# One block of 512 columns for batch 0's two halves in the up layer's last chunk, and new ranks in the planner

## The chip, the cores and the metric

The kernel runs on one core of a Trainium2 chip. A core has a matrix engine (TensorE, PE in the rows; its weight loads are PEld), VectorE (DVE), ScalarE (ACT), GpSimd (POOL) and SyncE (SP), which issues most DMAs. Each engine takes its own queue of instructions in order and waits on semaphores for the others. The metric is the device time of one execution in microseconds (us), the median of several runs. One execution is profiled, and its rows are what the argument rests on.

## What is computed

The reference is attention with a decay, followed by two feed-forward layers, all in float32:

```python
scores = q @ k^T / sqrt(64) + cum[i] - cum[j]      # cum: running sum of log f; causal
attn = softmax(scores); x = attn @ v               # 4 batches, 8 heads, 576 positions, 64 wide
x = x.transpose(0, 2, 1, 3).reshape(2304, 512)
x = (x @ w_a * (x @ w_b)) @ w_out                  # 512 -> 1536 -> 512: the up and down layers
h = x @ w_in                                       # 512 -> 1024
solu = h * softmax(h); ln = (solu - mean) / sqrt(var + 1e-6) * g_ln
out = ln @ w_out2                                  # 1024 -> 512
```

The kernel reaches float32 accuracy by parts: most operands are split into a high and a low part, and three products (high with high, low with high, high with low) are added in PSUM.

## The kernel before

**Stages.** The heads of batch 0 are worked in two passes, rows 0 to 255 of all 8 heads (kind `K0`) and then rows 256 to 575 (kind `K1`), so that the up layer can start on the first half early. The other 24 heads are whole (`KE` for the first two of batch 1, `KF` for the rest). Each head has: transposes of q and k (line 982), splits into high and low (lines 1003 to 1026), scores for the row maximum (line 1054) with a maximum on VectorE (line 1081 or 1084), the maximum turned into a row (lines 1099 and 1108), the scores with everything in them (line 1130), the exponential (ACT, lines 1192 and 1254) with the causal mask on GpSimd (line 1263), its split (lines 1272 and 1278), the product with v (lines 1215 and 1313) and the division by the sum (lines 1343 to 1378).

**The causal mask of the maximum.** For a head whose number is below `Y["PM"]` (and for all of `K0` and `K1`) TensorE adds the mask by a small bf16 matmul on each diagonal block (`ident` by `cmask`, line 1054), and VectorE takes a plain maximum (line 1081). For the others VectorE adds the mask and takes the maximum in one custom instruction and a read of its accumulator (line 1084).

**The up layer.** `STR` lists blocks of tokens: 0 and 1 are the two halves of batch 0 with 256 tokens each, 2 and 3 are 512 tokens of batches 1 and 2. For every block `i` and every chunk `c` of 128 of the 1536 features there is a unit (`up_unit`): 12 matmuls for `w_a` and 12 for `w_b`, on 256 or 512 columns, into two PSUM banks (line 1441); ACT copies the first out (line 1464), VectorE multiplies it with the second (line 1466), and SP stores the product to a DRAM tile `gs`. Units have a low rank, `key + Y["UK"]`: TensorE takes them where no attention work is ready. The 12 weight chunks are loaded, repaired (lines 699 to 715) and split (lines 737 and 742) before that. Batch 3, with the last 64 rows of every batch, goes through Strassen products instead ("group", line 1803, with prepared sums of weights, lines 1725 and 1732). Then come the down layer (`down`, line 2008), which loads `gs` again, and per pair of token blocks the last layers (lines 2096, 2162 to 2231 and 2241).

**The planner.** The order of all queues is not written out. Every operation is recorded with a rank (`key`) and the engines that may do it, and `Sched.run` plays a list schedule with rough costs: on each engine the ready operation of the lowest rank goes next, and where two or three engines may do it, the one that would end first, with a lean of so many us (`BIAS`, `BL`, `BS` ...). The ranks come from the table `Y`: shifts by head (`ZD`), by stage of a head (`KP`, `KN`), by weight (`WK`), and so on. `PN` is the first of the later layers' 28 weight blocks that is converted early and parked in DRAM.

**Fillers.** Where the planner's own schedule leaves TensorE a gap of more than `Y["FG"]` us, before `F1` = 640 us, a run of bf16 matmuls on constants is put into its queue (line 2321). Their number is the gap times `Y["FF"]` over the cost of one:

```python
if gap > Y["FG"] and place(at):
    todo.append((at, fill(gap * Y["FF"], *place(at), ...)))
```

Of the kernel before, what the change touches and what calls it, by code (L numbers as in the profile page):

```python
# [8 lines left out]
F32 = mybir.dt.float32  # L9
# [66 lines left out]
class Sched:  # L76
# [227 lines left out]
    "PN": 25,  # L304
    "KK": 265.3196,
    "KD": 15.1517,
    "TLD": 14.6185,
    "XP": -30.9366,
    "TO": 44.2857,
    "PA": 2.1045,  # L310
    "PS": 5.9662,
    "TK": 127.6384,
    "TD": 31.9136,
    "BT": -0.044,
    "UP": 434.967,
    "PG": 4.0796,
    "BP": -0.2335,
    "QK": 2,
    "TWK": 9.8272,
    "TWQ": 11.1039,  # L320
    "BK": -0.37,
    "BM": 0.9846,
    "Z0": 9.8683,
    "T0": 6.3669,
    "T1": 6.2527,
    "TA": 11.7627,
    "TF": 20.0998,
    "U0": 1.5861,
    "U1": 2.8457,
    "UF": 2.2924,  # L330
    "UL": 0.128,
    "LEAD": (1.2596, 5.9871),
    "SHRINK": 1.7818,
    "W0": 51.1769,
    "WD0": 5.2376,
    "WN": 3,
    "WD1": 0.0,
    "WD2": 15.5982,
    "EZ": 7.505,
    "EO": 20.0045,  # L340
    "TE": 28.4496,
    "DL": 0,
    "BIAS": 0.9425,
    "UO": (8.3054, 8.9928, 13.3396),
    "UD": 95.319,
    "UK": 380.0568,
    "L3": 18,
    "TL": (0.0, 0.0),
    "F1": 640.0,
    "FG": 0.3661,  # L350
    "FF": 0.7794,
# [3 lines left out]
    "YC": 17.6302,  # L355
    "T2": 11.7517,
    "TB": 1,
    "HB": 0,
    "F2": 181.8536,
    "LATE": 0.1776,  # L360
# [26 lines left out]
    "WIN": 0.0013,  # L387
# [4 lines left out]
def kernel(  # L392
# [48 lines left out]
          for i, (_, q0, q1) in enumerate(STR)]  # L441
    gsp = [dram.tile([P, 2 * TN], F32, name=f"gsp_{c}") for c in range(NF)]
# [986 lines left out]
    def up_unit(i, c, key, last):  # L1429
        b, q0, q1 = STR[i]  # L1430
        n_ = q1 - q0
# [3 lines left out]
        u[0].lo = 3 if i >= Y["L3"] else 2  # L1435
        uo = (0, n_) if len(u) == 1 else (0, 0)
# [14 lines left out]
        for j, (m, ks) in enumerate(parts):  # L1451
            rx = [(xsb[i][p], (s, p)) for p in ks for s in "hl"]
# [5 lines left out]
        aw = 2 * P if i < 2 else XT  # L1458
# [124 lines left out]
    def unit_plan(i, z0, dz):  # L1583
        for c in range(NF):
# [8 lines left out]
    unit_plan(0, xz[0] + 3.0, Y["U0"])  # L1593
# [776 lines left out]
```

## Time and profile before

| | us |
|---|---|
| median of 3 runs | 889.82 (889.47 to 891.45) |
| profiled execution, its own time | 887.92 |
| its span from the first to the last instruction | 886.04 |
| TensorE busy in it | 869.9 |
| fillers in that | 21.1 |

Rows name a line, an engine, an operation, what it writes and reads (tile names), its shape and its count. "[0.50 <-ACT xrw L1343]" says that the engine stood idle for 0.50 us before, and that ACT's instruction of line 1343 ended this. Matmuls overlap, so the distance of their starts is what one costs, and the time in a row is longer by the last one's own length.

### The profile page before, as it was taken

How to read it: one execution, taken by the hardware profiler on the slowest of the kernel's cores; microseconds unless marked ns; L12 is line 12 of the kernel's file. 1: busy time of each engine (PE TensorE's matmuls, PEld its weight loads, DVE VectorE, ACT ScalarE, POOL GpSimd, SP SyncE). 2: the span in 40 equal slices, each digit the busy share in tenths (PEclk: the TensorE clock that was granted, in tenths of full speed). 3: DMA queues.
4: the chain of work that ended last, by engine and by line, in shares of the span. 5: the costliest groups of instructions: out<-in, count | busy, mean ns of one | idle time of the engine just before them, and what ended most of it. 6: DMA issues, size and time to landing. Idle time of an engine off the chain costs nothing.

```text
span 886.0 us, 14300 instructions
## 1 busy us (share of the span) xinstructions
PE 869.9 (98%) x4899; PEld 755.7 (85%) x4899; DVE 676.4 (76%) x1305; ACT 444.9 (50%) x856; POOL 295.4 (33%) x440
## 2 busy tenths in 40 slices
PE   7999999999999999999999999999999999999997
PEld 5788989998888888888899987888888888888886
DVE  7988778789878867764788899887785666668774
ACT  3798755655654545444445556643532443344243
POOL 5666757656534533122234341112110010003001
PEclk9999999999999999999999999999999999999999
DMA  4476844445454453121276656421111212111001
GB/s 104 125 207 191 225 123 129 126 122 133 118 152 122 133 155 92 55 71 49 93 247 224 217 176 228 150 68 55 53 48 48 73 36 71 37 38 52 20 25 36
DMA packets 113356, 98.02 MB, mean 111 GB/s; under 512 B 69730, under 2 KB 92900, under 8 KB 113284
## 3 DMA queue, kind: packets, MB, share of 16 engines
q1 hardware_dynamic: 111396, 96.37, 36.9%
q10 hardware_dynamic: 1888, 0.75, 0.4%
q8 instruction: 38, 0.62, 0.3%
q14 instruction: 34, 0.28, 0.1%
HBM read 64.33 MB, written 26.49 MB: 103 GB/s over the span
## 4 chain that ended last, share of the span: by engine, by line
PE 87%; DVE 7%; ACT 2%; issue 2%; DMA 1%; POOL 0%; SPq 0%; DVEq 0%; ACTq 0%
PE ps L1441 20%; PE ps L2008 17%; PE ps L2241 10%; PE ps L2096 9%; PE ps L1803 9%; PE ps L1313 6%; PE ps L1130 5%; PE ps L1054 3%; PE ps L1215 3%; PE ps L2225 2%; PE ps L982 2%; DVE sets L1026 1%; DVE mts L1081 1%; PE ps L2321 1%; DMA sets<-sets 1%
## 5 line engine op out<-in xcount | busy, mean ns | idle before, releaser
L1441 PE MATMUL ps<-xs,wt 128*128 128x256 f32 (+1 forms) x1152 | 221.8, 341 | 0.5 <-POOL wt L742 0.5
L1441 PEld LDWEIGHTS ps<-xs,wt 128*128 128x128 f32 x1152 | 177.9, 189 | 21.8 <-POOL wt L742 0.8
L2008 PE MATMUL ps<-xs,wt 128*128 128x512 f32 (+1 forms) x360 | 81.2, 372 | 0.6 <-DVE fw L1853 0.5
L2008 PE MATMUL ps<-VS,wt 128*128 128x512 f32 (+1 forms) x360 | 79.5, 370 | 0.0
L2241 PE MATMUL ps<-sets,pexp 128*128 128x512 f32 x238 | 73.5, 390 | 0.0
L2008 PEld LDWEIGHTS ps<-xs,wt 128*128 128x128 f32 x360 | 62.5, 188 | 12.6 <-DVE fw L1853 1.6
L2008 PEld LDWEIGHTS ps<-VS,wt 128*128 128x128 f32 x360 | 62.9, 188 | 11.3
L1130 PE MATMUL ps<-sets 128*128 128x288 f32 (+16 forms) x400 | 68.8, 309 | 1.5 <-DVE mts L1084 0.5
L1313 PE MATMUL ps<-pexp,VS 128*128 128x448 f32 (+4 forms) x396 | 64.3, 311 | 0.0
L1130 PEld LDWEIGHTS ps<-sets 128*128 128x128 f32 (+2 forms) x400 | 58.3, 191 | 5.8 <-DMA sets<-sets 1.1
L1084 DVE CUSTOM_DVE_ANT_0 ps<-ps,cmask 128x512 f32<-128x512 f32 (+4 forms) x110 | 59.0, 553 | 5.3 <-PE ps L1054 2.3
L1263 POOL TENSOR_SCALAR_AFFINE_SELECT fw<-fw 128x128 f32<-128x128 f32 (+1 forms) x120 | 35.1, 322 | 80.5 <-ACT fw L1254 80.3
L1313 PEld LDWEIGHTS ps<-pexp,VS 128*128 128x128 f32 x396 | 58.7, 190 | 3.1 <-DVE pexp L1278 0.2
L1254 ACT ACTIVATE fw<-ps 128x768 f32<-128x768 f32 (+1 forms) x48 | 40.0, 838 | 26.1 <-PE ps L1130 24.9
L2241 PEld LDWEIGHTS ps<-sets,pexp 128*128 128x128 f32 x238 | 44.3, 188 | 9.0
L2241 PE MATMUL ps<-sets,xs 128*128 128x512 f32 x119 | 46.3, 389 | 0.0
L1054 PE MATMUL ps<-sets 66*128 66x512 f32 (+4 forms) x192 | 42.9, 323 | 3.3 <-DMA sets<-xs 1.7
L1272 ACT CAST pexp<-fw 128x768 fp32r<-128x768 f32 (+1 forms) x44 | 37.5, 859 | 14.4 <-POOL fw L1263 11.5
L2096 PE MATMUL ps<-wt,VS 128*128 128x512 f32 x162 | 44.3, 391 | 0.0
L1278 DVE TENSOR_TENSOR pexp<-fw,pexp 128x768 fp32r<-128x768 f32 (+1 forms) x35 | 36.2, 1043 | 9.1 <-ACT pexp L1272 8.8
L2109 DVE TENSOR_TENSOR xrw<-ps,xrw 128x512 f32<-128x512 f32 x34 | 23.5, 690 | 24.0 <-PE ps L2096 24.0
L1464 ACT COPY fw<-ps 128x256 f32<-128x256 f32 (+1 forms) x48 | 23.0, 479 | 37.3 <-PE ps L1441 31.4
(278 smaller groups left out, 1870.8 us busy)
## 6 DMA issues: line engine op xcount, KB each, us to landing
fw<-in_moe_w_out_dram SPq DMA_DIRECT2D x16, 512.0 KB
tdr<-fw SPq DMA_DIRECT2D x12, 512.0 KB
gs<-fw SPq DMA_DIRECT2D x24, 256.0 KB
sets<-sets SPq DMA_DIRECT2D x42, 144.0 KB
xrw<-tdr SPq DMA_DIRECT2D x11, 512.0 KB
fw<-in_moe_w_a_dram SPq DMA_DIRECT2D x10, 512.0 KB
fw<-in_moe_w_b_dram SPq DMA_DIRECT2D x10, 512.0 KB
nat<-in_k_dram SPq DMA_DIRECT2D x35, 128.0 KB
```

The source lines that it names most:

```text
L1054: nc.tensor.matmul(bank(ms[part], o, w), lhsT=a, rhs=b, start=o // 512 not in opened, stop=stop, skip_group_check=True)
L1084: nc.vector.tensor_tensor_reduce(out=x, in0=x, in1=cmask[:n, off:off + w], scale=1.0, scalar=-3.0e38, op0=ALU.add, op1=ALU.max, accum_out= ...
L1130: nc.tensor.matmul(bank(ss[i], o, w), lhsT=a, rhs=b, start=o // 512 not in opened, stop=stop, skip_group_check=True)
L1254: op(("ACT", t_act(n, True)), key + K.rk[4] + 5.5 + 0.9 * i, lambda i=i, n=n, pf=pf: nc.scalar.activation(out=pf(), in_=bank(ss[i], K.base ...
L1272: op(("ACT", t_act(n)), key + K.rk[5] + 6.8 + 0.9 * i, lambda bh=bh, n=n, pf=pf: nc.scalar.copy(out=pexp[:, 64 * bh.slot:64 * bh.slot + n] ...
L1278: o.fn = lambda o=o, bh=bh, bl=bl, n=n, pf=pf: ENG[o.eng].tensor_tensor(out=pexp[:, 64 * bl.slot:64 * bl.slot + n], in0=pf(), in1=pexp[:, ...
L1313: nc.tensor.matmul(bank(u, K.uo + q0, q1 - q0), lhsT=V[:, vp], rhs=src[:, o:o + q1 - q0], start=(k_ in K.first and ip == 0), stop=(k_ in K ...
L1441: nc.tensor.matmul(bank(u[m % len(u)], uo[m], n_), lhsT=wv(m, wp, c)[:, kk], rhs=xsv(i, xx, kk), start=(kk == 0 and n == 0), stop=(kk == K ...
L1803: nc.tensor.matmul(bank(bk, 0, TN), lhsT=operand(w, wp, kk), rhs=xb(x, xp)[:, kk], start=(first and kk == 0 and n == 0), stop=(kk == 1 and ...
L2008: nc.tensor.matmul(bank(py[d], 0, n), lhsT=WO[c][0][:, wp * DM:(wp + 1) * DM][:, ds_], rhs=ghv(gb, gp)[:, :n], start=(c == 0 and i == 0), ...
L2096: nc.tensor.matmul(bank(bk, 0, 512), lhsT=yc(yx, yp)[:, kk], rhs=wi(wx, wp, kk), start=(n == 0), stop=(n == 5))
L2241: nc.tensor.matmul(bank(po, 0, DM), lhsT=(zhv, zhv, zlv)[i][:, c], rhs=w2(c, (0, 1, 0)[i]), start=(c == 0 and i == 0), stop=(c == NF2 - 1 ...
```

## The change

**The wide block.** With `CM` = 11, the units of blocks 0 and 1 are made for chunks 0 to 10 alone. Chunk 11 of both is one unit with `i` = -1 and 512 columns: its moving operand `xsm` takes both halves of the split x in one access, its product goes to a new DRAM tile `gsm`, and the down layer's chunk 11 of batch 0 reads this by one DMA in place of two. It is planned behind the last weighing of the `KE` heads, since its 512-column buffers lie where these keep their data.

**The table.** Nearly all ranks and leans are new. Four entries do more than shift: `PM` 10 to 11 (head 10 gets its mask on TensorE), `PN` 25 to 26 (one weight block fewer is converted early), and `FG` 0.3661 to 0 with `FF` 0.7794 to 0.8938 (every gap gets fillers, and a larger share of it). `L3` and `HB` change too, but no operation reads them differently.

```diff
 Y = {
+    "CM": 11,
-    "PN": 25,
+    "PN": 26,
...
-    "UK": 380.0568,
+    "UK": 405.8544,
...
-    "FG": 0.3661,
-    "FF": 0.7794,
+    "FG": 0.0,
+    "FF": 0.8938,
...
-    "PM": 10,
+    "PM": 11,
...
+    gsm = [dram.tile([P, XT], F32, name=f"gsm_{c}") for c in range(NF)]
...
+    def xsm(part, p):
+
+        o = 2 * 2 * P * p + part * 2 * P
+        return xs[:, :2 * XH].rearrange("p (a x) -> p a x", a=2)[:, :, o:o + 2 * P]
...
     def up_unit(i, c, key, last):
-        b, q0, q1 = STR[i]
-        n_ = q1 - q0
+        both = i < 0
+        n_ = XT if both else STR[i][2] - STR[i][1]
...
-                        bank(u[m % len(u)], uo[m], n_), lhsT=wv(m, wp, c)[:, kk], rhs=xsv(i, xx, kk),
+                        bank(u[m % len(u)], uo[m], n_), lhsT=wv(m, wp, c)[:, kk],
+                        rhs=xsm(xx, kk) if both else xsv(i, xx, kk),
...
-        af = K1W + KEW + UPS if i == 2 else ()
+        af = K1W + KEW + UPS if both or i == 2 else ()
+        to = gsm[c] if both else gs[i][c]
...
-    unit_plan(0, xz[0] + 3.0, Y["U0"])
-    unit_plan(1, max(xz[1] + 3.0, xz[0] + 3.0 + 12 * Y["U0"]), Y["U1"])
+    CM = int(Y["CM"])
+    unit_plan(0, xz[0] + 3.0, Y["U0"], range(CM))
+    zm = max(xz[1] + 3.0, xz[0] + 3.0 + 12 * Y["U0"])
+    unit_plan(1, zm, Y["U1"], range(CM))
+    NKE = sum(1 for _, K in JOBS if K is KE) * len(KE.wei)
+    zk = max([Z[j] + Y["UO"][2] for j, x in enumerate(JOBS) if x[1] is KE] + [zm])
+    unit_plan(-1, zk + 0.02, Y["U1"], range(CM, NF))
...
+    merged = [(lambda c: gsm[c], XT, (-1,))]
...
-            for pi, (src, w, parts) in enumerate(blocks[j]):
+            bl = merged if j == 0 and c >= CM else blocks[j]
+            for pi, (src, w, parts) in enumerate(bl):
```

What it does to the queues is seen at three places. The lines after the change lie 7 to 17 higher for the same code (1441 is now 1449, 1054 is 1061, 2321 is 2338).

**TensorE, where the up layer goes from 256 to 512 columns** (some 205 us into the span). `xs` is the split x, `wt` the weights, `sets` the split q and k, `pexp` and `VS` the weights and v of a head. Before:

```order
L1441 MATMUL ps<-xs,wt 128x256 x6
L1313 MATMUL ps<-pexp,VS 128x128 x3
L1313 MATMUL ps<-pexp,VS 128x448 x3
L1313 MATMUL ps<-pexp,VS 128x192 x3
L1441 MATMUL ps<-xs,wt 128x256 x6
L1441 MATMUL ps<-xs,wt 128x512 x6
L1108 MATMUL ps<-ident,mts 7x128
L1054 MATMUL ps<-sets 128x512
L1054 MATMUL ps<-sets 128x384
L1054 MATMUL ps<-sets 128x128
```

and now:

```order
L1061 MATMUL ps<-sets 128x512
L1449 MATMUL ps<-xs,wt 128x512 x6
L1061 MATMUL ps<-sets 128x256 x2
L1061 MATMUL ps<-sets 128x320
L1061 MATMUL ps<-sets 128x384
L1061 MATMUL ps<-sets 128x128
L1449 MATMUL ps<-xs,wt 128x512 x12
L1320 MATMUL ps<-pexp,VS 128x128 x3
L1320 MATMUL ps<-pexp,VS 128x448 x3
L1320 MATMUL ps<-pexp,VS 128x192 x3
L1115 MATMUL ps<-ident,mts 7x128
L1449 MATMUL ps<-xs,wt 128x512 x6
```

Before, the last narrow matmuls are followed by the first of batch 1; now the narrow ones end earlier, and the 24 wide ones of chunk 11 (6, 12 and 6) stand between the scores and the products of heads, ahead of batch 1's.

**ACT, around 35 us**, in the pass from the first half's heads to the second's: line 1355 copies a head's result out of PSUM, line 1020 makes the high part of the next head's q. Before:

```order
L1003 CAST sets<-ps 64x576
L1363 ACTIVATE xrw<-xrw 128x256
L1366 ACTIVATE xrw<-xrw 128x256
L1355 COPY xrw<-ps 64x256
L1020 ACTIVATE sets<-ps 64x320
L699 ACTIVATE fw<-fw 128x512
```

and now (line 1027 is 1020, line 1362 is 1355):

```order
L1010 CAST sets<-ps 64x576
L1370 ACTIVATE xrw<-xrw 128x256
L1373 ACTIVATE xrw<-xrw 128x256
L1027 ACTIVATE sets<-ps 64x320
L1362 COPY xrw<-ps 64x256
L706 ACTIVATE fw<-fw 128x512
```

The high part of q stands ahead of the copy.

**TensorE, the scores for the maximum of head 10** (`cmask`, `ident`: the mask as a matmul). Before:

```order
L1054 MATMUL ps<-sets 128x512
L1054 MATMUL ps<-sets 128x384
L1054 MATMUL ps<-sets 128x128
L1054 MATMUL ps<-sets 128x256 x2
L1054 MATMUL ps<-sets 128x320
L1130 MATMUL ps<-sets 128x448 x2
L1130 MATMUL ps<-sets 128x64 x2
```

and now, from the second of its score matmuls on:

```order
L1061 MATMUL ps<-sets 128x384
L1061 MATMUL ps<-sets 128x128
L1061 LDWEIGHTS ident
L1061 MATMUL ps<-cmask,ident 128x128
L1061 LDWEIGHTS ident
L1061 MATMUL ps<-cmask,ident 128x128
L1061 MATMUL ps<-sets 128x256 x2
L1061 MATMUL ps<-sets 128x320
L1061 LDWEIGHTS ident
L1061 MATMUL ps<-cmask,ident 128x128
L1061 LDWEIGHTS ident
L1061 MATMUL ps<-cmask,ident 128x64
```

Five mask matmuls, one on each diagonal block (four are in these rows), with their loads of `ident`, stand between the scores.

Fillers are 107 matmuls before and 136 now. In the part of the queue that took the first 45 us before there are 67 of them before (8 of 512 columns, 48 of 352, 11 of 256) and 86 now (9, 61 and 16); behind it 40 before and 50 now, all of 352 columns. The first 330 rows of TensorE's queue, fillers aside, are the same but for two swaps.

## Rows read from the trace of the kernel before

**Rows 1.** The page's part 1: busy us, share, instructions by engine.
```profile
PE 869.9 (98%) x4899; PEld 755.7 (85%) x4899; DVE 676.4 (76%) x1305; ACT 444.9 (50%) x856; POOL 295.4 (33%) x440
```

**Rows 2.** Stages: length, busy us (instructions) by engine, granted clock, DMA share, GB/s.
```profile
0.00:45.00 45.00, 38.88 (x266) 28.94 (x267) 37.70 (x90) 25.33 (x58) 27.00 (x68) 1.00 0.47 118
45.00:110.00 65.00, 64.90 (x480) 58.29 (x480) 53.15 (x84) 54.69 (x107) 46.15 (x53) 1.00 0.75 207
110.00:440.00 330.00, 326.91 (x1973) 290.85 (x1972) 247.39 (x495) 174.91 (x288) 148.32 (x228) 1.00 0.39 110
440.00:560.00 120.00, 118.00 (x634) 109.00 (x633) 104.68 (x180) 62.91 (x129) 40.55 (x52) 1.00 0.66 218
560.00:866.00 306.00, 306.00 (x1483) 256.78 (x1482) 224.93 (x445) 120.06 (x262) 30.45 (x30) 1.00 0.17 53
866.00:886.00 20.00, 15.17 (x73) 11.85 (x72) 8.57 (x16) 7.00 (x14) 2.88 (x10) 1.00 0.15 39
```

**Rows 3.** The same stages, instructions of line 2321 alone: the fillers; their sum.
```profile
0.00:45.00 45.00, 13.77 (x67) 6.63 (x67) 1.00 0.47 118
...
sum 886.00, PE 21.11 PEld 10.07; mean PE 3.52 PEld 1.68
```

**Rows 4.** TensorE's waits from 45 us on: us in total, times, longest.
```profile
PE ps L1803 <- ACT fw L1818: 0.8, 2, 0.6
PE ps L1803 <- ACT nat L1818: 0.6, 1, 0.6
PE ps L1108 <- DVE mts L1084: 0.5, 1, 0.5
```

**Rows 5.** The chain that ended last: start us, us, what.
```profile
100.46 2.88 PE ps L1441 x24
...
418.22 19.06 PE ps L1441 x84
```

**Rows 6.** Timeline of TensorE (start us, us, instruction, count), 24 and 36 us.
```profile
24.13 0.29 PE L1054 MATMUL ps<-cmask,ident 128*128 128x128 bf16 x2
24.25 0.61 PE L2321 MATMUL ps<-cmask,ident 128*128 128x352 bf16 x3
24.60 0.74 PE L1130 MATMUL ps<-sets 128*128 128x256 f32 x2
...
36.22 0.47 PE L1054 MATMUL ps<-sets 66*128 66x512 f32 x1 [0.32 <-ACT sets L1020]
...
37.30 0.68 PE L1130 MATMUL ps<-sets 128*128 128x256 f32 x4
```

**Rows 7.** Timeline of TensorE at fillers and at what waits behind them.
```profile
1.58 3.59 PE L2321 MATMUL ps<-fw 128*128 128x512 bf16 x8 [1.58 <-DVE fw L600]
...
11.70 0.41 PE L1054 MATMUL ps<-sets 66*128 66x256 f32 x2 [1.22 <-DMA sets<-xs]
...
27.68 0.48 PE L1215 MATMUL ps<-xrw,fw 128*128 128x256 f32 x1 [0.50 <-ACT xrw L1343]
...
214.42 1.80 PE L2321 MATMUL ps<-cmask,ident 128*128 128x352 bf16 x11
216.77 0.28 PE L1108 MATMUL ps<-ident,mts 128*7 128x128 f32 x1 [0.54 <-DVE mts L1084]
```

**Rows 8.** Timeline of ACT, then of VectorE, around 36 us.
```profile
35.23 0.35 ACT L1355 COPY xrw<-ps 64x256 f32<-64x256 f32 x1
35.60 0.43 ACT L1020 ACTIVATE sets<-ps 64x320 fp32r<-64x320 f32 x1
...
37.27 2.21 DVE L1081 TENSOR_REDUCE mts<-ps 128x1 f32<-128x512 f32 x4
```

**Rows 9.** Line 1278, the weights' low part: ns min/median/max by engine; who waited.
```profile
L1278 DVE TENSOR_TENSOR pexp<-fw,pexp x35: 937/960/2110, 194.7 to 412.4; 128x768 fp32r<-128x768 f32 x18, 128x832 fp32r<-128x832 f32 x17
L1278 POOL TENSOR_TENSOR pexp<-fw,pexp x9: 1840/1976/2430, 141.0 to 263.2; 128x832 fp32r<-128x832 f32 x5, 128x768 fp32r<-128x768 f32 x4
...
  PEld ps L1313: 0.2, 1
```

More of the change, by code (lines that the diff above doesn't have):

```diff
@@ L303 @@
 Y = {
-    "PN": 25,
[L305 to L317, printed above, removed]
+    "CM": 11,
+    "PN": 26,
+    "KK": 270.7605,
+    "KD": 7.4836,
+    "TLD": 44.641,
+    "XP": -33.9844,
+    "TO": 33.4945,
+    "PA": 3.7788,
+    "PS": 6.9662,
+    "TK": 125.7673,
+    "TD": 25.9632,
+    "BT": 0.4352,
+    "UP": 490.4727,
+    "PG": 4.3039,
+    "BP": -0.1796,
     "QK": 2,
[L319 to L322, printed above, removed]
+    "TWK": 9.2301,
+    "TWQ": 11.1928,
+    "BK": -0.5486,
+    "BM": 2.007,
     "Z0": 9.8683,
-    "T0": 6.3669,
+    "T0": 6.3613,
     "T1": 6.2527,
[L326 to L333, printed above, removed]
+    "TA": 11.3754,
+    "TF": 20.4882,
+    "U0": 4.3197,
+    "U1": 3.1238,
+    "UF": 3.1294,
+    "UL": 0.115,
+    "LEAD": (1.0045, 6.0026),
+    "SHRINK": 1.9624,
     "W0": 51.1769,
-    "WD0": 5.2376,
+    "WD0": 5.3804,
     "WN": 3,
     "WD1": 0.0,
[L338 to L341, printed above, removed]
+    "WD2": 15.1641,
+    "EZ": 5.4926,
+    "EO": 19.3535,
+    "TE": 27.6762,
     "DL": 0,
-    "BIAS": 0.9425,
-    "UO": (8.3054, 8.9928, 13.3396),
-    "UD": 95.319,
-    "UK": 380.0568,
-    "L3": 18,
+    "BIAS": 0.272,
+    "UO": (9.165, 9.5642, 13.3819),
+    "UD": 83.7544,
+    "UK": 405.8544,
+    "L3": 19,
     "TL": (0.0, 0.0),
     "F1": 640.0,
-    "FG": 0.3661,
-    "FF": 0.7794,
+    "FG": 0.0,
+    "FF": 0.8938,
     "RA": 1,
@@ L354 @@
     "HC": 2,
-    "YC": 17.6302,
-    "T2": 11.7517,
+    "YC": 17.8892,
+    "T2": 11.9796,
     "TB": 1,
-    "HB": 0,
-    "F2": 181.8536,
-    "LATE": 0.1776,
[8 rows of a table removed]
+    "HB": 2,
+    "F2": 157.493,
+    "LATE": 0.1817,
[8 rows of a table added]
     "XL": -0.4279,
[4 rows of a table removed]
[4 rows of a table added]
     "PO": 1,
[1 row of a table removed]
[1 row of a table added]
     "KE": 1,
@@ L380 @@
     "NB": 145000.0,
[1 row of a table removed]
[1 row of a table added]
     "TW": 1,
[1 row of a table removed]
[1 row of a table added]
     "MM": 1,
[2 rows of a table removed]
-    "WIN": 0.0013,
[2 rows of a table added]
+    "WIN": 0.001,
 }
@@ L1435, in up_unit @@
         u[0].lo = 3 if i >= Y["L3"] else 2
+        assert not both or len(KEW) == NKE
         uo = (0, n_) if len(u) == 1 else (0, 0)
@@ L1451, in up_unit @@
         for j, (m, ks) in enumerate(parts):
-            rx = [(xsb[i][p], (s, p)) for p in ks for s in "hl"]
+            rx = [(xsb[x][p], (s, p)) for x in ((0, 1) if both else (i,)) for p in ks for s in "hl"]
             rw = [(WB[c], ((m, k_), s)) for k_ in ks for s in "hl"]
@@ L1457, in up_unit @@
         gt = s_.buf("gt")
-        aw = 2 * P if i < 2 else XT
+        aw = 2 * P if 0 <= i < 2 else XT
         atv = lambda: AG[:, :n_]
         gtv = lambda: AG[:, aw * (1 + gt.slot):aw * (1 + gt.slot) + n_]
-        af = K1W + KEW + UPS if i == 2 else ()
+        af = K1W + KEW + UPS if both or i == 2 else ()
+        to = gsm[c] if both else gs[i][c]
         fs = len(s_.ops)
@@ L1468, in up_unit @@
            r=[(u[-1], 1), (at, 0)], w=[(gt, 0)], after=af)
-        op(("SP", 0.44), key - 50.0, lat=1.45, fn=lambda: issue(out=gs[i][c], in_=gtv()),
+        op(("SP", 0.44), key - 50.0, lat=1.45, fn=lambda: issue(out=to, in_=gtv()),
            r=[(gt, 0)], w=[(GD, (i, c))], nbytes=512.0 * n_)
-        if i < 2:
+        if 0 <= i < 2:
             UPS.extend(s_.ops[fs:])
@@ L1581, with unit_plan @@
         stages(j)
-    def unit_plan(i, z0, dz):
-        for c in range(NF):
+    def unit_plan(i, z0, dz, cs=range(12)):
+        for c in cs:
             at_(z0 + dz * c, lambda i=i, c=c: up_unit(i, c, z0 + dz * c, i >= B))
@@ L1994, in down @@
                 o += w
-            rr = [(gr, x) for x in range(len(blocks[j]))]
+            rr = [(gr, x) for x in range(len(bl))]
             op(("ACT", t_act(n)), key - 3.0, lambda gr=gr, gb=gb: nc.scalar.copy(
```

32 rows, old and new, of the table Y are left out of this document.

## The prediction, made before the changed kernel ran

> **What bounds the kernel now.** I read the page's first part, then a table of stages, then the waits of TensorE. TensorE is busy 869.9 of 886.0 us [rows 1], and the granted clock is 1.00, its level of 2.4 GHz, in every stage [rows 2]. So the time is what stands in TensorE's queue, plus the places where the queue stands still. The stages differ much [rows 2]. From 0 to 45 us TensorE is idle for 45.00 - 38.88 = 6.1 us: this is the chain of the first heads. From 45 to 110 it is idle for 0.1 us, from 110 to 440 for 3.1 us, from 440 to 560 for 2.0 us, from 560 to 866 not at all, and in the last 20 us for 4.8 us (the last rows' norm and store). Part of the busy time is no work: the filler matmuls that the code sets into gaps, 13.8 us before 45 us and 21.1 - 13.8 = 7.3 us after [rows 3]. So all that a better order could still find between 45 and 866 us is 5.2 us of idle time and at most 7.3 us of fillers. There no single wait of TensorE is over 0.6 us [rows 4].
>
> **The merge.** Chunk 11 of the up layer is 48 matmuls of 256 columns, 24 for each half of batch 0; it becomes 24 of 512. In the chain, 24 matmuls of 256 columns take 2.88 us, 0.120 us each, and 84 of 512 columns take 19.06 us, 0.227 us each [rows 5]. A pair of halves costs 0.240 us, one wide matmul 0.227 us, so the merge saves 24 x 0.013 = 0.31 us. Its bounds are 0 (the switch of weights hides it) and 0.6 us (twice that, since with one unit fewer a change of form goes too). The page "TensorE: Matmul & The Clock Gate" of the Trainium skill, section "Back-to-back issue gap", puts the isolated gap at columns over 2.4 GHz plus 2.5 ns; by it the merge would save an estimated 24 x 2.5 ns = 0.06 us. The rows have about 13 ns a matmul above the column time, so I stay with them; either way the step is too small to be measured.
>
> Around it, ACT loses two copies of 256 columns and gains one of 512, VectorE two products for one, and SP two stores and two loads for one each. From 110 to 440 us ACT is busy 53% and VectorE 75% [rows 2]; TensorE's queue of up units hides this, and I count nothing. The wide block must wait until both halves and the two first heads of batch 1 are done, so it stands just ahead of the batch-1 units, where the last narrow units and the first wide one stood. Up to 110 us the same number of up matmuls stands in TensorE's queue, so nothing is starved. If that cover failed, 24 x 0.227 = 5.4 us of stuffing would be missing in the attention; but from 45 to 110 us TensorE idles for 0.1 us only, since other units stand ready.
>
> **One more head with masks on TensorE.** The table's limit for masks goes from 10 to 11, so head 10 gets five small mask matmuls, and five fused mask-and-max instructions of VectorE become plain maxima. Two mask matmuls stand 0.12 us ahead of what follows them [rows 6], 0.06 us each or 0.3 us for five. Where masks stand between wide matmuls, three of them and 1408 columns take 37.30 - 36.22 = 1.08 us [rows 6], of which the columns at the pace of rows 5 are some 0.63 us: 0.15 us each, 0.75 us for five. I take +0.5 us. What VectorE saves lies in a stage where TensorE doesn't wait for it, and counts nothing.
>
> **More fillers.** There are 107 before and 136 after: 19 more in the first part (1 of 512 columns, 13 of 352, 5 of 256) and 10 of 352 behind it. Eleven of 352 columns span 1.80 us, so one takes at most 0.16 us; I use 0.15 us, 0.12 us for 256 columns (the pace of rows 5), and 3.59 / 8 = 0.45 us for one of the eight of 512 [rows 7]. That is 0.45 + 13 x 0.15 + 5 x 0.12 + 10 x 0.15 = 4.5 us of TensorE. What covers them is the wait that still follows a run of fillers now: 1.22 us for a DMA at 11.7 us, 0.50 us at 27.7, 0.54 us at 216.8 [rows 7]. Five of the new ones (0.45 + 4 x 0.15 = 1.05 us) stand ahead of the first of these and are free. But behind the run at 24.25 us the next matmul follows without a wait [rows 6], and there each new filler pushes what follows. Between 0 and 3.4 us I take +0.5 us, near the low end, because most runs grow at places that still wait. The clock gains nothing by them: it is at 1.00 already [rows 2].
>
> **The first 45 us otherwise** keep their order but for a few swaps. ACT makes the high part of q (0.43 us) ahead of a copy of 0.35 us [rows 8], and TensorE's next scores waited 0.32 us for this [rows 6]. That could give back 0.32 us; but VectorE, which takes the maxima of these scores, takes four of them in a row from 37.27 to 39.48 us [rows 8] and is the later of the two, so most of it is lost again at the next maximum. I take -0.1 us, between -0.3 and 0.
>
> **The rest of the ranks.** Behind 110 us the attention's pieces and the up units stand in another order. Five subtractions for the low part of the attention's weights go from GpSimd (about 1.98 us each) to VectorE (about 0.96 us), nine small subtractions of the weight sums go the other way, and one weight block fewer is converted early and parked in DRAM. TensorE's weight loads wait 0.2 us in all for those first subtractions now [rows 9], so faster ones shorten a wait that hardly exists. The block's conversion moves to a place around 560 us; behind that TensorE doesn't idle [rows 2], so it is hidden, and without that cover it would cost the 0.7 us or so of one 512-column VectorE step. What the new order does to the 5.1 us of idle time from 110 to 560 us no row shows. Its bounds are -5.1 us, all of it gone, and +3.1 us, the idle time of 110 to 440 us once more. I take a quarter gone, -1.2 us: a new order hides old waits and makes some new ones. The group products keep their order for two thirds of their rows, and the last 20 us keep all of it, so there I count nothing.
>
> **The sum** is -0.31 + 0.5 + 0.5 - 0.1 - 1.2 = -0.6 us. The profiled execution took 887.92 us (886.04 us span and 1.88 us around it), and the median of the runs is 889.82 us, 1.90 us above it. Put on the median the forecast is 889.2 us. A measurement here can tell some 0.2%, 1.8 us, from no change, so this lies inside "the same".
>
> **Rivals.** *The ranks do the work* (faster). They take 3 of the 5.1 us of idle time and 0.5 us of the first part's chain, with the fillers covered: -0.31 + 0.5 - 0.5 - 3 = -3.3 us, 886.5 us. For it: the waits are many, short and for several engines [rows 4], which an order can shift. Against it: the fillers behind 45 us, which stand where the planner sees a gap, rise from 40 to 50. *The fillers push* (slower). If none of the new ones but the five at the start is covered, the term is +3.4 instead of +0.5 us; with nothing from the ranks (0 instead of -1.2 us) the sum is +3.5 us, 893.3 us. It decides from 1.7 us of uncovered fillers, with the ranks at nought. For it: the run at 24.25 us has no wait behind it. Against it: three runs with 2.3 us of waits behind them [rows 7]. *The new order waits where the old didn't* (slower), above all at the hand-over from the group products to the down layer, at 530 to 570 us, where 18 fillers become 23: +3 instead of -1.2 us gives +3.6 us, 893.4 us. *The merge doesn't save*: 889.5 us, inside the forecast.
>
> **How the numbers follow.** The forecast, with the merge that saves nothing, has 0.43 (its own range is 888.1 to 891.5 us), the ranks 0.37, the pushing fillers 0.11, the new waits 0.09. That gives faster 0.37, the same 0.43, slower 0.20. The range must take in most of both sides: 885.3 to 892.3 us leaves out the far parts of the ranks' case and of the slower ones, some 2 in 10.
>
> **What would show it.** In the new profile: 24 up matmuls of 512 columns more and 48 of 256 fewer, at 0.227 us each; idle time of TensorE from 110 to 560 us near 4 us (near 2 us: the ranks do the work; above 6 us: new waits); smaller waits behind the fillers of the first 45 us, and the first wide score still at about 36.2 us (over 0.5 us later: the fillers push); the stretch from the first down product to the end the same within 0.5 us. I am wrong if the stretch from 570 us on changes, since I count nothing there, or if the first 110 us move by more than 1 us.

## The result, and the profile after

The changed kernel is slower: **895.45 us** (median of 6 runs, 893.13 to 898.15) against 889.73 us (889.47 to 891.45), a ratio of 1.0056 with an interval of 1.0040 to 1.0072. Run once more beside the experiments it took 895.35 us against 889.97 us, 1.0053 (1.0035 to 1.0072). The forecast was 889.2 us and "the same"; the time lies above the range. The merged block is not the cause. Three things are: waits that the new order makes, fillers that push, and a clock that falls.

Its profiled execution took 898.15 us, with a span of 896.4 us. The page's line for TensorE (busy time, share of the span, instructions), which answers to [rows 1]:

```profile
PE 878.7 (98%) x4909; PEld 760.9 (85%) x4909; DVE 684.9 (76%) x1304; ACT 442.9 (49%) x857; POOL 291.0 (32%) x433
```

The stages of TensorE's time, as in [rows 2] (stretch, its length, busy time of each engine with instructions, granted clock, DMA share and GB/s):

```profile
0.00:45.00 45.00, 38.77 (x265) 29.12 (x266) 36.59 (x86) 23.70 (x54) 24.39 (x67) 0.96 0.45 105
45.00:110.00 65.00, 64.24 (x469) 56.95 (x469) 51.92 (x81) 54.67 (x108) 44.98 (x52) 1.00 0.72 200
110.00:440.00 330.00, 326.32 (x1941) 288.42 (x1940) 249.06 (x481) 171.22 (x287) 145.04 (x220) 0.99 0.40 109
440.00:560.00 120.00, 118.15 (x644) 109.91 (x644) 99.99 (x181) 57.98 (x121) 39.81 (x55) 1.00 0.63 202
560.00:866.00 306.00, 305.96 (x1481) 256.31 (x1480) 230.74 (x451) 127.09 (x273) 33.89 (x32) 1.00 0.20 62
```

TensorE's busy share is 98% again, and its idle time from 110 to 560 us is 3.68 + 1.85 = 5.5 us where before had 5.1. A reader who stops at this idle time sees half a microsecond of the 10 us between the two profiled spans. The column of the clock shows more: 0.96 and 0.99 where every stage of before had 1.00. Cut finer, the same view finds the places; two of three are shown, the third begins at 38.93 us:

```profile
200.00:202.80 2.80, 2.02 (x13) 1.60 (x12) 2.58 (x8) 1.34 (x2) 1.22 (x4) 0.99 0.67 148
202.80:206.20 3.40, 3.40 (x11) 2.75 (x10) 1.14 (x3) 2.47 (x3) 1.76 (x5) 0.50 0.27 106
206.20:210.00 3.80, 3.80 (x21) 3.30 (x21) 3.55 (x9) 0.50 (x1) 1.62 (x1) 1.00 0.11 44
285.00:288.10 3.10, 1.52 (x11) 1.35 (x11) 3.07 (x5) 1.15 (x2) 2.94 (x3) 1.00 0.44 99
288.10:291.50 3.40, 3.40 (x11) 2.81 (x10) 2.99 (x10) 0.00 (x0) 2.77 (x3) 0.50 0.00 0
291.50:295.00 3.50, 3.50 (x20) 3.01 (x19) 1.19 (x2) 0.00 (x0) 0.46 (x1) 1.00 0.09 33
```

Three times, for 3.41 us each, the granted clock is 0.50, which is 1.2 GHz instead of 2.4. TensorE is fully busy there and does 11 matmuls in 3.40 us, where the stretches behind have 21 in 3.80 us and 20 in 3.50 us. A drop costs half its length, 1.7 us, and three cost 5.1 us: 898.15 - 5.1 = 893.0 us. The one run of the first six that had no drop (mean clock 0.999) took 893.13 us. Ahead of each drop stands a wait. The waits of TensorE behind 45 us (waited for: us in total, times, longest us), which answer to [rows 4]:

```profile
PE ps L1320 <- DVE pexp L1285: 2.0, 3, 1.6
PE ps L1818 <- DVE fw L1842: 0.7, 1, 0.7
PE ps L1137 <- ACT xrw L1362: 0.7, 1, 0.7
```

The first is new in kind: no wait of [rows 4] is over 0.6 us. It stands at 287 us. The timeline of TensorE there, then that of VectorE (start, length, what, idle time before and what ended it):

```profile
285.49 0.34 PE L1320 MATMUL ps<-pexp,VS 128*128 128x128 f32 x2
287.40 1.72 PE L1320 MATMUL ps<-pexp,VS 128*128 128x128 f32 x7 [1.58 <-DVE pexp L1285]
```

```profile
284.71 0.69 DVE L1740 TENSOR_TENSOR fw<-wt 128x512 f32<-128x512 f32 x1 [1.34 <-DMA tdr<-fw]
285.32 2.03 DVE L1285 TENSOR_TENSOR pexp<-fw,pexp 128x768 fp32r<-128x768 f32 x1
```

TensorE waits for the subtraction that makes the low part of the attention's weights. VectorE took it late, because a step of the prepared weight sums (L1740) stood ahead of it in its queue and waited 1.34 us for a store, which frees its buffer. In the kernel before the two stood the other way round there, the subtraction (L1278) ahead of the weight step (L1725), and nobody waited:

```profile
275.00 0.96 DVE L1278 TENSOR_TENSOR pexp<-fw,pexp 128x768 fp32r<-128x768 f32 x1 [0.65 <-ACT pexp L1272]
...
279.03 0.68 DVE L1725 TENSOR_TENSOR fw<-wt 128x512 f32<-128x512 f32 x1
```

The wait of 0.7 us at 201 us is also one of order: VectorE's step of the division by the sums (L1352) stands behind a split of q (L1033), ScalarE's copy (L1362) waits for it, and TensorE's scores (L1137) wait for that copy.

Fillers, which answer to [rows 3], first the part up to 45 us and then the sum of all stages:

```profile
0.00:45.00 45.00, 17.44 (x85) 8.74 (x85) 0.96 0.45 105
...
sum 866.00, PE 27.47 PEld 13.18; mean PE 5.49 PEld 2.64
```

They took 27.5 us where they took 21.1. And the first wide score, which the forecast wanted at about 36.2 us as in [rows 6], starts at 37.48 us. The timeline shows no gap between the nine fillers and the up unit at 35.11 us; the unit's second part then waits for a converted weight block, and the score for its turn:

```profile
36.30 0.85 PE L1449 MATMUL ps<-xs,wt 128*128 128x256 f32 x5 [0.79 <-POOL wt L749]
37.48 0.47 PE L1061 MATMUL ps<-sets 66*128 66x512 f32 x1 [0.32 <-issue]
```

### The profile page after: what moved, and what is told of

The parts are those of the page before. It is cut to its first block, busy times and chain, and to the rows that moved or that the text cites. A ratio compares the mean times of both kernels' runs of the same rounds, so it can differ in the third digit from the quotient of the medians.

```text
span 896.4 us, 14285 instructions
## 1 busy us (share of the span) xinstructions
PE 878.7 (98%) x4909; PEld 760.9 (85%) x4909; DVE 684.9 (76%) x1304; ACT 442.9 (49%) x857; POOL 291.0 (32%) x433
## 4 chain that ended last, share of the span: by engine, by line
PE 85%; DVE 8%; DMA 3%; ACT 3%; issue 1%; POOL 0%; SPq 0%; DVEq 0%; ACTq 0%
PE ps L1449 20%; PE ps L2025 16%; PE ps L2258 9%; PE ps L1818 9%; PE ps L2113 9%; PE ps L1320 6%; PE ps L1137 5%; PE ps L1061 3%; PE ps L1222 2%; PE ps L2242 2%; DMA fw<-in_moe_w_a_dram 2%; PE ps L989 1%; PE ps L2338 1%; DVE pexp L1285 1%; DMA tdr<-fw 1%
## 5 line engine op out<-in xcount | busy, mean ns | idle before, releaser
L1449 PE MATMUL ps<-xs,wt 128*128 128x512 f32 (+1 forms) x1128 | 224.3, 348 | 1.1 <-POOL wt L749 0.8
L2025 PE MATMUL ps<-xs,wt 128*128 128x512 f32 (+1 forms) x360 | 81.3, 372 | 0.0
L1137 PE MATMUL ps<-sets 128*128 128x288 f32 (+16 forms) x400 | 67.1, 307 | 1.5 <-ACT xrw L1362 0.7
L1091 DVE CUSTOM_DVE_ANT_0 ps<-ps,cmask 64x576 f32<-64x576 f32 (+4 forms) x105 | 56.4, 552 | 15.7 <-PE ps L1061 13.1
L1270 POOL TENSOR_SCALAR_AFFINE_SELECT fw<-fw 128x128 f32<-128x128 f32 (+1 forms) x120 | 39.2, 356 | 76.7 <-ACT fw L1261 76.4
L1137 PEld LDWEIGHTS ps<-sets 128*128 128x128 f32 (+2 forms) x400 | 57.9, 191 | 5.1 <-ACT xrw L1362 0.9
L1285 DVE TENSOR_TENSOR pexp<-fw,pexp 128x768 fp32r<-128x768 f32 (+1 forms) x40 | 43.8, 1104 | 7.4 <-ACT pexp L1279 6.9
L1061 PE MATMUL ps<-sets 66*128 66x512 f32 (+2 forms) x192 | 44.2, 333 | 2.6 <-DMA sets<-xs 1.9
L749 POOL TENSOR_TENSOR wt<-fw,wt 128x512 fp32r<-128x512 f32 (+1 forms) x30 | 35.7, 1193 | 21.7 <-ACT wt L744 20.7
L1474 ACT COPY fw<-ps 128x512 f32<-128x512 f32 (+1 forms) x47 | 22.8, 484 | 36.8 <-PE ps L1449 35.3
```

Source lines behind the costliest of these rows:

```text
L1061: nc.tensor.matmul(bank(ms[part], o, w), lhsT=a, rhs=b, start=o // 512 not in opened, stop=stop, skip_group_check=True)
L1091: nc.vector.tensor_tensor_reduce(out=x, in0=x, in1=cmask[:n, off:off + w], scale=1.0, scalar=-3.0e38, op0=ALU.add, op1=ALU.max, accum_out= ...
L1137: nc.tensor.matmul(bank(ss[i], o, w), lhsT=a, rhs=b, start=o // 512 not in opened, stop=stop, skip_group_check=True)
L1270: nc.gpsimd.affine_select(out=x, in_=x, pattern=[[1, w]], base=0, channel_multiplier=-1, compare_op=ALU.is_ge, fill=0.0)
L1285: o.fn = lambda o=o, bh=bh, bl=bl, n=n, pf=pf: ENG[o.eng].tensor_tensor(out=pexp[:, 64 * bl.slot:64 * bl.slot + n], in0=pf(), in1=pexp[:, ...
L1449: nc.tensor.matmul(bank(u[m % len(u)], uo[m], n_), lhsT=wv(m, wp, c)[:, kk], rhs=xsm(xx, kk) if both else xsv(i, xx, kk), start=(kk == 0 a ...
```

## The experiments

All are compared with the kernel before on the same chip: over four sets its median was 890.69, 889.97, 890.25 and 890.58 us. Each run also reports its mean granted clock. Runs at 0.999 or 1.000 are called "at full clock" below (the clock falls at the very end of all kernels, behind the last matmul), and their median is given beside the median of all. The kernel before took 890.05 us at full clock (61 of 98 runs).

### The fillers, put back and put in

The changed kernel with the old filler settings, and the kernel before with the new ones:

```diff
-    "FG": 0.0,
-    "FF": 0.8938,
+    "FG": 0.3661,
+    "FF": 0.7794,
```

> The changed kernel in its new order, with the filler settings of the kernel before: 88 fillers of 352 columns, 11 of 256 and 8 of 512 instead of 110, 16 and 9; nothing else moves. Theory 1 (two causes: the new order waits in new places, and behind its longer waits the granted clock falls to 1.2 GHz for 3.4 us at a time): fewer fillers give back little of the +5.7 us or make it worse, 894.5 to 898 us, and the trace shows at least one stretch of clock 0.5. Rival 2 (the fillers push): the 4.5 us of new fillers are most of the loss, and 891 to 892.5 us comes out.

(The changed kernel has 111 fillers of 352 columns; 110 is the count of the next kernel.) Measured: 891.95 us, 1.0014 (1.0005 to 1.0024), and 890.66 us at full clock (4 of 12 runs), mean clock 0.9971.

> The kernel before in its old order, with the changed kernel's filler settings, so more fillers in the same gaps; nothing else moves. Rival 2 (the fillers push): 892 to 893.5 us. Theory 1 (order and clock): within 1 us of the kernel before, 889 to 890.7 us, and the granted clock stays at 1.00.

Measured: 892.39 us, 1.0016 (1.0006 to 1.0027), every run at full clock.

In both, the rival "the fillers push" came out, and my first theory, which gave them nothing, fell. (The drop that it expected is in the trace of the first, at 14.07 us.) Put into the old order they cost 1.9 us at full clock, against the 890.47 us that the kernel before takes so on the same chip. But the clock also speaks: with the new fillers the old order held it in every run, its own mean on that chip being 0.998. So fillers do two things, and the theory from here on has both.

### The merge, taken apart in its place

```diff
-                    nc.tensor.matmul(
-                        bank(u[m % len(u)], uo[m], n_), lhsT=wv(m, wp, c)[:, kk],
-                        rhs=xsm(xx, kk) if both else xsv(i, xx, kk),
...
+                    w_ = 2 * P if both else n_
+                    for h in range(n_ // w_):
+                        nc.tensor.matmul(
+                            bank(u[m % len(u)], uo[m] + h * w_, w_), lhsT=wv(m, wp, c)[:, kk],
+                            rhs=xsv(h, xx, kk) if both else xsv(i, xx, kk),
...
```

> The changed kernel with the wide block's 24 matmuls of 512 columns issued as 24 pairs of 256 columns into the same bank, in the same place of the same order. It prices the merge alone by the span of the block in the trace: by the rows of before, 24 x 0.227 = 5.4 us become 48 x 0.120 = 5.8 us, +0.31 us; if weight loads hide the difference, +0.06 us or nothing. The time as a whole can't tell 0.3 us. Rival 3 (the wide block itself costs the time, because it makes the attention wait): a time of 891 us or less and other waits of TensorE.

Measured: 892.91 us in one run, at a clock of 1.000. The block's three pieces, first split, then whole (from the run with plugs at 201 and 286 us, whose clock was 1.000 there too):

```profile
200.82 1.58 PE L1451 MATMUL ps<-xs,wt 128*128 128x256 f32 x12
202.87 3.08 PE L1451 MATMUL ps<-xs,wt 128*128 128x256 f32 x24
207.06 1.68 PE L1451 MATMUL ps<-xs,wt 128*128 128x256 f32 x12
```

```profile
201.01 1.53 PE L1449 MATMUL ps<-xs,wt 128*128 128x512 f32 x6
...
203.00 2.96 PE L1449 MATMUL ps<-xs,wt 128*128 128x512 f32 x12
...
207.08 1.63 PE L1449 MATMUL ps<-xs,wt 128*128 128x512 f32 x6
```

6.34 against 6.12 us: the merge saves 0.22 us. (Each of the six rows is 0.16 us longer than the distance from its start to the next instruction's, so the difference stands.) The rows of before had given 0.31 us [rows 5]. The estimate from the Trainium skill's page "TensorE: Matmul & The Clock Gate", section "Back-to-back issue gap", was 0.06 us; the measurement lies between the two and nearer to the rows. Whether the block's place costs anything this run can't show, since it keeps the place.

### Plugs in the long waits

A plug is a run of fillers set directly ahead of a named step of TensorE; the numbers are places in its queue.

```diff
+    plug = {40: 0.95, 253: 0.75, 338: 1.5}
+    for n, o in enumerate(o for o in order if o.eng == PE):
+        if n in plug:
+            todo.append((o.start, fill(plug[n], *place(o.start - 0.01), False)))
```

> The changed kernel with 18 more fillers of 352 columns, set directly ahead of the three matmul groups where the profiled run waited longest behind 35 us: five ahead of the up unit at 35.1 us, four ahead of the scores at 201.7 us and nine ahead of the weighted sums at 286 us. They lie inside waits of 0.8 to 1.6 us, so they cost next to nothing. Theory 1 (the clock falls behind these waits): the drops at 39, 203 and 288 us are gone, the clock is 0.999 or better and the time is 892 to 893.5 us, 2 to 3 us less than the changed kernel. If the waits aren't what lets the clock fall: drops remain, 895 to 898 us. If fillers push: 897 us or more with the clock at 1.00.

Measured: 893.16 us, 1.0031 (1.0020 to 1.0041), all runs at full clock. Beside the next three, the changed kernel itself was run again, and the plugs were parted:

> The changed kernel itself, unedited, beside the three that follow. On its first runs it took 895.45 us where its mean clock was 0.997; its copy with 18 plugging fillers took 893.16 us at 0.999. Theory 1 (clock falls behind the longer waits, in some places of some runs): 894 to 896 us, a mean clock below that of the plugged kernels, and runs at a clock of 0.999 or 1.000 take 892.5 to 893.5 us. Rival (the drops of the first six runs were chance, and the plugs did nothing): the same clock and time as the plugged kernels, 893 us.

Measured: 895.35 us; mean clock 0.997, no run at full clock, so what such runs take stays untested here. The profiled one (893.45 us) has a single drop, at 200.27 us.

> The changed kernel with five fillers of 352 columns more, directly ahead of the up unit at 35.1 us, which waits there for a weight block that GpSimd converts; nothing at the two other places. If this wait is the one behind which the clock falls in most runs: clock 0.999, 893 us. If the later two count as much: about 894.5 us and a clock between that of the unplugged and of the fully plugged kernel.

Measured: 893.94 us, 1.0037 (1.0023 to 1.0052), mean clock 0.998, 3 of 9 runs at full clock; those three took 891.46 us in the median.

> The changed kernel with four fillers ahead of the scores at 201.7 us and nine ahead of the weighted sums at 286 us, none at 35 us: the counterpart of the run before. If the wait at 35 us is what lets the clock fall in most runs: 894.5 to 895.5 us, with a drop at about 39 us in the trace. If the two later waits do: 893 us.

Measured: 893.50 us, 1.0038 (1.0022 to 1.0054), all 7 runs at full clock. The same two stretches, first with the plug at 35 us alone, then with those at 201 and 286 us:

```profile
199.40:202.80 3.40, 3.40 (x11) 2.81 (x10) 1.10 (x4) 2.47 (x3) 1.57 (x4) 0.50 0.38 154
...
284.70:288.10 3.40, 3.40 (x11) 2.81 (x10) 2.82 (x9) 0.00 (x0) 2.60 (x3) 0.50 0.00 0
```

```profile
199.40:202.80 3.40, 3.31 (x19) 2.75 (x18) 2.31 (x9) 2.58 (x4) 2.07 (x6) 1.00 0.15 34
...
284.70:288.10 3.40, 3.40 (x19) 2.88 (x18) 2.98 (x10) 0.00 (x0) 2.54 (x3) 1.00 0.00 0
```

Where the waits are filled, the clock holds; where they are open, it falls behind them. It doesn't always: the second run of the changed kernel waited 1.4 us at 284 us without a drop there. But in none of the profiled runs did a drop stand without a wait of 0.5 us or more shortly ahead of it. The wait at 35 us matters less than the two later ones.

The drop is one thing, the wait another. 893.2 to 893.5 us is still 3 us above the kernel before: all the new fillers are there, and a plug fills a wait and doesn't shorten it. The next run has the plugs with the old fillers behind 16 us.

```diff
-            if gap > Y["FG"] and place(at):
-                todo.append((at, fill(gap * Y["FF"], ...
+            if gap > (0.0 if at < 16.0 else 0.3661) and place(at):
+                todo.append((at, fill(gap * (0.8938 if at < 16.0 else 0.7794), ...
```

> The changed kernel's order with the old, fewer fillers behind 16 us, the new ones up to there, and the three plugs: the fillers that push are gone, those in long waits are there. Theory: fillers' push (2 us) and clock (2 us or more) add up and both come back: 890.3 to 891.2 us at a clock of 0.999 or better, level with the kernel before. If the plugs push as other fillers do: 892 us or more.

Measured: 892.21 us, 1.0017 (1.0003 to 1.0031), 11 of 13 runs at full clock: 1 us over the upper end, and in the band of the other case, that plugs push as other fillers do. I had counted the clock and the fillers and forgotten the waits; but the waits alone don't explain it. The changed kernel with the old fillers and no plugs (and eight fillers fewer up to 16 us) has the same order and took 890.66 us at full clock, 1.5 us less; with all the new fillers and the plug at 35 us alone it took 891.46 us, against 893.50 us with the other two plugs. These are medians of four and three runs, and a run without a drop may also be one with short waits. So that the plugs are free isn't shown, and the 893.2 us may hold something of their own price.

For the waits change from one execution to the next. In the profiled run with the split block, which has the same order and no plug, VectorE's weight step (L1742 there) didn't wait for its store, the subtraction took half as long, and TensorE's weighted sums followed without a wait:

```profile
279.96 0.69 DVE L1742 TENSOR_TENSOR fw<-wt 128x512 f32<-128x512 f32 x1
280.57 1.04 DVE L1285 TENSOR_TENSOR pexp<-fw,pexp 128x768 fp32r<-128x768 f32 x1
```

Another wait, which no edit here touched, comes and goes too: at 62 to 64 us TensorE waits for an exponential on ScalarE, ahead of which a step waits for the load of a weight block. It was under 0.2 us in the second run of the changed kernel and 1.88 us in the profiled run of this one, with a drop at 64.79 us behind it:

```profile
64.35 2.10 PE L1222 MATMUL ps<-fw,xrw 128*128 128x320 f32 x4 [1.88 <-ACT nat L1199]
```

### The two waits, mended at their cause

Two steps of VectorE move forward by a place; TensorE's queue is unchanged.

```diff
-    todo += [(o.start, lambda o=o: emit(o)) for o in order]
+    early = {1543: 1541, 1166: 1162}
+    todo += [(order[early[n]].start - 0.001 if n in early else o.start, lambda o=o: emit(o))
+             for n, o in enumerate(order)]
```

> The changed kernel with two steps of VectorE moved forward and nothing else: the subtraction for the attention's weights ahead of the weight conversion that waits at 280 us for a store, and the scaled copy of the sums at 197 us ahead of one row step of the keys. They are what TensorE's two longest waits behind 45 us go back to (1.4 to 1.6 us before the weighted sums at 284 us, 0.7 us before the scores at 199 us). Theory 1: both waits go, with them the drops of the clock at about 200 and 286 us, and no filler is needed for it: clock 0.999 and 891 to 892.5 us. If those waits lie there for another reason (the port, the store itself): they stay within 0.3 us, and 894 to 896 us.

Measured: 892.08 us, 1.0019 (1.0007 to 1.0031), 891.31 us at full clock (6 of 12 runs), mean clock 0.998. VectorE's two steps, and TensorE behind them:

```profile
280.86 0.96 DVE L1285 TENSOR_TENSOR pexp<-fw,pexp 128x768 fp32r<-128x768 f32 x1 [0.30 <-ACT pexp L1279]
281.74 0.68 DVE L1740 TENSOR_TENSOR fw<-wt 128x512 f32<-128x512 f32 x1
```

```profile
282.69 1.42 PE L1320 MATMUL ps<-pexp,VS 128*128 128x128 f32 x9
```

The long wait is gone, and so is its drop; the weight step (the "weight conversion" of the expectation), now second, doesn't wait for its store any more, so the swap costs VectorE no wait. At 198 us the theory failed: the wait is not gone but stands one step earlier (0.96 us, before the scores for the row maximum, for the same copy by ScalarE), and the clock still fell at 200.05 us in the profiled run. (What the expectation calls a row step of the keys is the split of q.)

```profile
198.32 0.70 PE L1061 MATMUL ps<-sets 66*128 66x512 f32 x3 [0.96 <-ACT xrw L1362]
```

With the old filler settings as well (the first diff, on top of this one):

> The run before with the old filler settings as well (88 of 352 columns instead of 111): the changed kernel's order and merge, its two new waits mended and its new fillers taken back. If new waits with their drops and pushing fillers are all of the loss: 889.3 to 890.7 us, within 0.1% of the kernel before, at a clock of 0.998 or better. If the rest of the order or the merged block costs something of its own: 891.5 us or more.

Measured: 891.69 us, 1.0014 (1.0000 to 1.0028); 889.89 us at full clock (5 of 12 runs), mean clock 0.998. At full clock the whole loss is gone: 889.9 us against 890.1 us of the kernel before on that chip. Nothing is left for the merge, the masks and the rest of the order, within what such medians can tell. How the loss divides is less sure. By the steps 893.2 (plugs only), 891.3 (wait mended), 889.9 (fillers back), the wait cost 1.9 us and the fillers 1.4 us; by the steps 893.1 (the changed kernel's one run at full clock), 890.7 (fillers back), 889.9 (wait mended), the fillers cost 2.5 us and the wait 0.8 us. The median of all twelve runs misses the forecast by a microsecond and lies just above the 891.5 us that the expectation gave to a further cost; seven of the runs had drops again: the old fillers hold the clock less well.

### The same on the kernel before

Its late fillers are switched off by one number.

```diff
-    "F1": 640.0,
+    "F1": 110.0,
```

> The kernel before, in its own order, without its 40 fillers of 352 columns behind 110 us; nothing else moves. Three claims are tested. If fillers behind 110 us hold the clock, it now falls behind waits that they covered (at about 122, 217 or 535 us), the mean clock is below that of the kernel before, and the time is 890.5 to 893 us. If they only push, their 6 us of TensorE, of which most lies in waits, give back 0.5 to 1.5 us with the clock as it was: 888.5 to 889.5 us. If both, the two cancel within 1 us and only the clock shows it.

Measured: 890.83 us, 0.9998 (0.9985 to 1.0011). At full clock 889.23 us (4 of 12 runs), and the mean clock 0.9970. So both effects are there and cancel: 0.9 us less of pushing (890.10 us at full clock for the kernel before on that chip), and drops in two runs of three. The waits of TensorE from 110 to 560 us show what was uncovered; the first had been 0.54 us behind its eleven fillers [rows 7], and the profiled run has a drop at 219.37 us, behind it:

```profile
PE ps L1108 <- DVE mts L1084: 2.4, 2, 2.2
PE ps L2008 <- DVE fw L1853: 1.9, 2, 1.6
PE ps L1803 <- ACT fw L1818: 1.7, 2, 1.2
```

### The merge with the old ranks

The changed code, with the whole table of the kernel before and `"CM": 11`, planned anew.

> The merge alone: the changed kernel's code with every number of the old table, planned anew (so the old numbers act on a list of work that is one block shorter, and the order of other steps shifts by itself; fillers 105, 11 and 8). If the merge is worth its 0.3 us and harmless: 889 to 891 us. If the wide block's later start makes the attention wait (it stands behind both halves and two heads): 892 us or more with new waits of TensorE between 60 and 150 us.

Measured: **905.34 us**, 1.0171 (1.0152 to 1.0191), mean clock 0.991: far above the first expectation, and in the open range of the second, but not by its waits. They are everywhere, not between 60 and 150 us (110 to 440 us has 6.2 us of idle time, 440 to 560 us 5.4 us), and the clock fell at five places in the profiled run, at two of them for 6.83 us:

```profile
0.00:45.00 45.00, 38.51 (x240) 29.01 (x241) 36.04 (x85) 23.37 (x53) 25.78 (x68) 0.89 0.45 106
...
110.00:440.00 330.00, 323.80 (x1925) 287.16 (x1924) 244.15 (x477) 163.69 (x265) 136.68 (x217) 0.98 0.40 111
440.00:560.00 120.00, 114.56 (x612) 104.25 (x611) 105.20 (x198) 62.15 (x136) 44.73 (x54) 0.99 0.60 195
```

So the time isn't that of the merged block's matmuls, which cost less, and the waits that its place was to make didn't come. What remains is an order for which the old numbers don't fit; this is argued, since no run parts it from what the merge does to the planning. Against this run the new ranks are worth 10 of the 15 us.

### Fillers only where something waits

The order with the two swaps and the old filler settings, in which 15 fillers that no wait follows are taken out and 44 are added inside waits (numbers of TensorE's queue, with their counts):

```diff
+    count = {4: 30, 7: 5, 20: 6, 24: 4, 26: 0, 30: 6, 35: 0, 40: 10, 251: 6,
+             538: 8, 553: 0, 590: 6, 591: 10, 595: 0, 611: 0}
...
+            if n in count:
+                todo.append((at, fill(count[n] * 0.16 + 0.001, *place(at), False)))
+            elif gap > Y["FG"] and place(at):
```

> The changed kernel's order with the two VectorE steps moved forward and the old fillers, of which the 15 that no wait follows are taken out (runs of three at 24.5, 30.2, 492, 544 and 570 us) and 44 are added where the trace shows a wait of 0.4 to 1.7 us still open (9.6, 13, 20, 27, 34, 196, 474, 531 and 534 us). Theory: fillers cost time only where nothing waits, and hold the clock only where something does. Then both effects come in: the time at full clock falls by 0.5 to 1 us below the 889.9 us of the run before it, and the mean clock rises from 0.998 to 0.999 or more: 888.8 to 889.8 us. If a filler inside a wait costs time as well (it delays what comes when the wait is shorter): 890.5 us or more at the better clock.

Measured: **888.87 us**, 0.9974 (0.9961 to 0.9987), all 11 runs at full clock. Both numbers came in: 1.0 us less than the run before it at full clock, and a clock of 0.9995. This version beats both kernels, the kernel before by 0.26% (its interval ends at 0.9987) and the changed one by 0.7%. Its stages behind 110 us have 1.6 and 0.7 us of idle time:

```profile
110.00:440.00 330.00, 328.39 (x1961) 289.97 (x1960) 250.10 (x487) 172.31 (x289) 147.56 (x222) 1.00 0.39 108
440.00:560.00 120.00, 119.31 (x650) 111.28 (x649) 103.13 (x185) 62.31 (x128) 39.77 (x52) 1.00 0.66 212
```

On the kernel before, in the same manner, with places of its own:

> The same aim on the kernel before, whose order stays: 19 of its fillers that no wait follows are taken out (at 22.2, 24.3, 30.0, 490, 530, 559 and 568 us) and 32 are added in waits that its trace shows (10, 13, 20, 27, 34, 216, 474 and 533 us). Theory: 1 us less at full clock (its late fillers alone cost 0.9 us) and a clock of 0.999: 888.7 to 889.7 us, 0.1% below the kernel before. If fillers inside waits cost time as well: 890.5 us or more.

Measured: 890.59 us, 0.9993 (0.9979 to 1.0008), and 890.47 us at full clock (11 of 12 runs). The clock came as expected, the time at full clock didn't fall, and the second case, that fillers inside waits cost time as well, came in by 0.1 us. So that a filler inside a wait is always free isn't shown: in this order something of the 32 added ones, or of the runs' own scatter (888.38 to 892.98 us), took back what the 19 gave. Which of them did so stays open; the wait at 62 us, under 0.2 us in the profile of the kernel before, is 0.48 us in this one.

## Why the prediction was wrong

**The clock** is the step of the prediction that failed outright: "The clock gains nothing by them: it is at 1.00 already [rows 2]". It is read off one execution, 887.92 us, which is faster than any of the 98 timed ones. Of these, 24 had a mean clock under 0.997 and took 892.6 us in the median. The clock at 1.00 was kept up by fillers and short waits; it was not a given. What drops cost the changed kernel is the difference between 895.4 us and the 893.2 us with plugs, some 2.2 us (for the kernel before 890.4 - 890.05, 0.3 us). The mean clocks, 0.9969 over its twelve runs and 0.9994 with plugs, give the same: 0.0025 x 893 = 2.2 us.

**The rest of the ranks**, -1.2 us, had the wrong sign. Its term was idle time alone, and of the idle time from 110 to 560 us it hoped for a quarter less, near 4 us; the profiled run had 5.5 us. Mending the wait at 285 us was worth 0.8 to 1.9 us at full clock (the one at 201 us only moved), and such waits bring drops besides. The forecast looked at which engine does the subtractions and how long one takes, and said that their wait "hardly exists" [rows 9]. What it left out is what stands ahead of them in VectorE's queue: a weight step that itself waits for a store. The bound of +3.1 us on this term would have held it.

**The fillers**, +0.5 us between 0 and 3.4: mis-sized. They cost 891.3 - 889.9 = 1.4 us in the new order with the wait mended, 893.1 - 890.7 = 2.5 us with it open, and 1.9 us in the old order. "Most runs grow at places that still wait" was the wrong weight: the run at 24 us has none behind it, and of the ten fillers added behind 45 us most stand where nothing waits for them.

**Right:** the merge's size (0.22 us measured for 0.31), that nothing is starved by it (as far as 889.9 against 890.1 us can tell), and the stretch from 570 us on, where the first matmul of x w_in and the last matmul of all are 315.9 us apart, 316.3 before. From the first down product on, where the list of signs allows 0.5 us, it is 365.9 us against 368.7: this sign failed, since the first down product comes later in the new order. The masks and the swaps of the first 45 us were not measured by themselves; with the merge and the remaining order they add up to -0.2 us (889.9 against 890.1). By its own list the prediction was wrong in the first 110 us: the hundredth up matmul starts at 90.6 us, 86.9 before, of which a drop of the clock is 1.7 us. In the second profiled run of the same kernel, without a drop there, it starts at 87.5 us, inside the 1 us of the list.

**The rivals** named two of the three causes, each alone: the pushing fillers (893.3 us) and the new waits (893.4 us, put at the hand-over at 530 to 570 us, where they were not; they stand at 201 and 286 us). Each alone forecast about the 893.2 us of the plugged kernel, which has no drops; measured, the two share that loss, so the near match is luck. That they could come together, and that waits cost the clock as well, had no case and no chance.

## What to carry to other kernels

Read the granted clock and the longest waits over several executions before calling them given: one profile at 1.00 doesn't say what a change will find. When an order changes, look at what each engine's queue holds ahead of the steps that the bounding engine needs, above all steps that wait for a DMA; swapping one such pair was worth more than the change's own gain. A filler belongs where the trace shows an open wait that stays, and a new order needs its fillers placed anew: this gained 1 us in the new order, and nothing at full clock in the old.

## What the runs showed of the hardware

- TensorE's clock falls to 1.2 GHz although the engine is 98% busy over the whole, behind single waits of 0.5 to 2.2 us. In the profiled runs a drop between the first and the last matmul lasted 3.41 us, or 6.83 us twice in one run; one of 3.41 us costs up to 1.7 us. The same wait is followed by a drop in some executions and not in others.
- The subtraction of 768 columns on VectorE that TensorE waits for at 285 us took 2.03 to 2.10 us in seven profiled runs of the new order and 0.96 to 1.05 us in four. In the seven, GpSimd's step of the weight sums (L1740, below in the profile of the changed kernel, where the subtraction starts at 285.32 us) had begun before it or with it; in the four it began later. The place in VectorE's queue doesn't decide it: the run with the split block kept the old place and has 1.04 us, and the run with the swap and the old fillers has 2.10 us.

```profile
284.82 1.71 POOL L1740 TENSOR_TENSOR fw<-wt 128x512 f32<-128x512 f32 x1 [1.12 <-DMA tdr<-fw]
```
